# Grouping the tiled attention matmuls of a Nystromformer + multiplicative FFN kernel, with two batches' hidden values in one tile

## Chip, cores and metric

The kernel runs on one core of one Trainium2 chip. The metric is device time in microseconds (us) of one execution; several executions are compared by their median.

## What is computed

The reference is an attention in Nystrom form over 8 batches, 8 heads, 576 positions and 64 channels, followed by a feed-forward net whose third and fourth weight are applied one after the other.

```python
q_lm, k_lm = means of q, k over groups of 18 positions      # 32 landmarks
A  = softmax(q    @ k_lm.T / 8)                              # 576 x 32
Bm = softmax(q_lm @ k_lm.T / 8)                              # 32 x 32
C  = softmax(q_lm @ k.T    / 8)                              # 32 x 576
Z  = Bm.T / (norm_1(Bm) * norm_inf(Bm) + 1e-6)
for _ in range(6):
    Z = 2 * Z - Z @ Bm @ Z
x  = (A @ Z @ C @ v)            # heads side by side: 4608 x 512
out = ((x @ w1) * (x @ w2) @ w3) @ w_out
```

Inputs and output are float32.

## The kernel before

**The stages.** `fold` multiplies w3 by w_out once into `w34` (64 products of three 128x512 matmuls each, L507, with transposes of w3 in between, L494). The attention of batch 0 is woven between these products. After that a loop over the eight batches `b` does two things at once: it applies the feed-forward net to batch b, and it advances the attention of batch b+1. The attention of a batch is never multiplied out to x. Instead `attention` folds Z C v into the up weights: it leaves `g` = (Z C v) w1 and w2 per head group (L430) and `ahat`, the normalised A, and `up` multiplies g by ahat.

**The feed-forward part of batch b.** For each of eight 128-row slices j of the hidden layer there are two calls of `up`: w = 0 (4 matmuls of 128x288, L444; ScalarE copies the result to `a_sb`, L448) and w = 1 (4 more; VectorE multiplies it by a_sb into `ab`, L450). `down` then takes 128 rows of ab at a time; a chunk is two halves of four 128x512 matmuls (L464), and after the second half ScalarE writes `o_sb` (L470) and SyncE sends it out. 576 rows are four and a half chunks: an even batch does four chunks, and the odd batch after it does five, the first from 64 rows of the batch before and 64 of its own, as two column tiles of 64.

**The attention as a generator.** `attention` yields after each step, and the main loop calls `steps(at, n)` to place a step behind a piece of feed-forward work. TensorE executes in program order, so this placing is a schedule written by hand (`manual_schedule`). In this document the steps are named so:

| name | what TensorE does | lines |
|---|---|---|
| L | landmark sums from `parts` into `psL`, then `lm` (ScalarE), `qbd` (VectorE) | L201, L206, L208 |
| B | landmark scores, then bm and bt on VectorE | L217 to L230 |
| C0, C1 | scores of k against q landmarks, exp to `ect`, row sums `es` on GpSimd (`presum`) | L242, L246, L253 to L258 |
| R, A0 | first product of the iteration and A scores of heads 0 to 3 | L306, L292 |
| A1, V0 | A scores of heads 4 to 7, C v of heads 0 to 3 | L292, L323 |
| V1 | C v of heads 4 to 7 | L323 |
| I0 to I5 | the six iterations; the row sums of A (`denominators`) in I1, their reciprocals in I2 to I4, `rmix` in I5 | L387 to L397, L349, L357, L364 |
| Z, N0 | last product, `zt`, and `normalise(0)` to ahat | L407, L412, L371, L374 |
| N1, G | `normalise(1)` and the four pieces of g, one for each step | L371, L430 to L436 |

In the loop, L of the next batch stands at the end of the iteration before; B to I1 follow the eight `up(j, 0)` one each; the rest follow the halves of `down`.

**Buffers in PSUM.** `big` is a pool of three two-bank tiles, used by up, scores, iterations, normalise, g and every second down chunk. `small` and `acc` are one bank each. `bank` is acc in the main loop and small for batch 0. The sums and reciprocals of A (`psS`) lie in a big tile from I1 to I5.

**Queues.** SyncE's queue holds, in order: `turn_all(b+2)` (four DMA transposes, L106) at the start of an iteration, four pieces of v (L85), each held until ScalarE has written one element of its target (L84), and the output DMAs (L477). GpSimd does `presum`, two small products (`bmn`, `bmbd`) and then `landmarks` of batch b+2 (L183 to L192), between whose operations it issues the loads of q and k of batch b+3 (`qk_pieces`). For batch 1 v is one load (`load_v`) and for batch 2 q and k are two (`load_qk`).

Of the kernel before, what the change touches and what calls it, by code (L numbers as in the profile page):

```python
# [15 lines left out]
S = 576  # L16
# [15 lines left out]
def kernel(  # L32
# [163 lines left out]
    def attention(st, bank=None):  # L196
# [145 lines left out]
        ahat = []  # L342
        psS = None

        def denominators():
            ps = big()
# [6 lines left out]
            return ps  # L353

        def inverted(i):
            sl = slice(QS // 3 * i, QS // 3 * (i + 1))
            nc.vector.reciprocal(out=psS[:, 1, sl], in_=psS[:, 0, sl])  # L357

        def mixed():
            rr = psS[:, 1, 0:QS]  # L360
# [7 lines left out]
        def normalise(qd, rmix):  # L368
            psD = big()
            for c in range(4):  # L370
                nc.tensor.matmul(psD[:, c // 2, QS * (c % 2):QS * (c % 2) + QS],  # L371
                                 selc[:, qd, c, :], rmix[:, :], start=True, stop=True)
            a = pat.tile([128, 2, HS], FP16, name="ahat", bufs=4)
            nc.vector.tensor_tensor(out=a, in0=eat[qd].rearrange("p (c s) -> p c s", c=2),  # L374
                                    in1=psD[:, :, 0:HS], op=ALU.mult)
            ahat.append(a)


        for it in range(6):
            last = it == 5  # L380
# [24 lines left out]
        psZ = small()  # L405
        for qd in range(2):
# [11 lines left out]
        st["ahat"] = ahat  # L418


        g = st["g"] = pat.tile([128, 2, 2, DF], FP16, name="gt")
        for n in range(2):
            for w in range(2):
                psG = big()
                fs = slice(512 * n, 512 * n + 512)
                for i in range(2):
                    for h in range(4):
                        for qd in range(2):
                            rs = slice(64 * qd, 64 * qd + 64)
                            nc.tensor.matmul(psG[32 * h:32 * h + 32, qd, :], zt[rs, i, h, :],  # L430
                                             wup[rs, h, w, fs], start=(i == 0), stop=(i == 1),
                                             tile_position=(64 * qd, 32 * h))
                if w == 0:
                    nc.scalar.activation(out=g[:, :, w, fs], in_=psG, func=AXF.Copy, scale=1.0 / ZS)  # L434
                else:
                    nc.vector.tensor_scalar(out=g[:, :, w, fs], in0=psG, scalar1=1.0 / ZS,  # L436
                                            scalar2=None, op0=ALU.mult)
                yield

    def up(st, j, w):  # L440
        p = big()
        for qd in range(2):
            for c in range(2):
                nc.tensor.matmul(p[:, c, 0:HS], st["g"][:, qd, w, 128 * j:128 * j + 128],  # L444
                                 st["ahat"][qd][:, c, :], start=(qd == 0), stop=(qd == 1))
        if w == 0:
            st["a_sb"] = po.tile([128, 2, HS], FP16, name="a_sb", bufs=2)
            nc.scalar.copy(out=st["a_sb"], in_=p[:, :, 0:HS])  # L448
        else:
            nc.vector.tensor_tensor(  # L450
                out=st["ab"][:, j, :].rearrange("p (c s) -> p c s", c=2),
                in0=st["a_sb"], in1=p[:, :, 0:HS], op=ALU.mult)


    rows = out.rearrange("(b p g) f -> b g p f", b=B, g=6)

    def down(srcs, half, hold, bank):
        if half == 0:
            hold["ps"] = bank()
        pso = hold["ps"]  # L460
        for j in range(4 * half, 4 * half + 4):
            o = 0
            for _, ab, s0, sz in srcs:
                nc.tensor.matmul(pso[o:o + sz, :], ab[:, j, s0:s0 + sz], w34[:, j, :],  # L464
                                 start=(j == 0), stop=(j == 7),
                                 tile_position=(0, o))
                o += sz
        if half == 1:
            o_sb = po.tile([128, DM], FP32, name="o_sb")
            nc.scalar.activation(out=o_sb, in_=pso[:, :], func=AXF.Copy,  # L470
                                 scale=1.0 / (X64 * X64))
            o = 0
            for b, _, s0, sz in srcs:
                while sz:
                    gi, p0 = divmod(s0, NP)
                    n = min(sz, NP - p0)
                    nc.sync.dma_start(out=rows[b, 2 * (gi % 3) + gi // 3, p0:p0 + n, :],  # L477
                                      in_=o_sb[o:o + n, :])
                    o, s0, sz = o + n, s0 + n, sz - n


    def fold(pf, wof, w3f, wsp, warm_up):
# [58 lines left out]
    with tc.tile_pool(name="pf", bufs=2) as pf:  # L541
# [64 lines left out]
        turn_all(1)  # L606
        steps(fd, 6)
        at = attention(sts[0])
        for n, m in enumerate((2, 2, 2, 2, 2, 2, 2, 1, 1, 1, 1, 1, 1, 1, 2, 2, 2, 2, 2, 1)):
            steps(at)  # L610
            if n == 1:
                load_w3(7)
                load_v(sts[1], 1)
            elif n == 4:
                landmarks(sts[1], 1)
                load_qk(sts[2], 2)
                landmarks(sts[1], 0)
            steps(fd, m)
        steps(at, 30)
        steps(fd, 64)  # L620
    pab = ctx.enter_context(tc.tile_pool(name="pab", bufs=3))
    at = attention(sts[1], acc)
    steps(at)


    for b in range(B):
        st = sts[b]
        ab = st["ab"] = pab.tile([128, 8, S], FP16, name="ab")
        if b + 2 < B:
            turn_all(b + 2)  # L630
        if b % 2 == 0:
            chunks = [[(b, ab, 128 * t, 128)] for t in range(4)]
        else:
            chunks = [[(b - 1, sts[b - 1]["ab"], 512, 64), (b, ab, 0, 64)]]
            chunks += [[(b, ab, 64 + 128 * t, 128)] for t in range(4)]
# [50 lines left out]
```

## Time and profile before

| what | value |
|---|---|
| median of 8 runs | 289.14 us (287.84 to 292.28) |
| the profiled execution | 290.02 us |
| its span, first to last instruction | 288.0 us |
| TensorE busy share of the span | 95% |
| VectorE, ScalarE, GpSimd | 58%, 46%, 53% |
| batch 0's `up` begins | 73.36 us after the span's start |
| batch 7's `up` begins | 265.87 us |

The profiled execution spends 2.0 us outside its span. A row of the timeline gives start and length in us, engine, line, operation, output and inputs, shapes and count; the bracket is the idle time before it and what ended it. A matmul's length includes its way through the array, so the cost of a group is read from the start of one group to the start of the next.

### The profile page before, as it was taken

How to read it: one execution, taken by the hardware profiler on the slowest of the kernel's cores; microseconds unless marked ns; L12 is line 12 of the kernel's file. 1: busy time of each engine (PE TensorE's matmuls, PEld its weight loads, DVE VectorE, ACT ScalarE, POOL GpSimd, SP SyncE). 2: the span in 40 equal slices, each digit the busy share in tenths (PEclk: the TensorE clock that was granted, in tenths of full speed). 3: DMA queues.
4: the chain of work that ended last, by engine and by line, in shares of the span. 5: the costliest groups of instructions: out<-in, count | busy, mean ns of one | idle time of the engine just before them, and what ended most of it. 6: DMA issues, size and time to landing. Idle time of an engine off the chain costs nothing.

```text
span 288.0 us, 9554 instructions
## 1 busy us (share of the span) xinstructions
PE 274.1 (95%) x4028; PEld 151.0 (52%) x4028; DVE 167.2 (58%) x430; ACT 131.8 (46%) x231; POOL 152.3 (53%) x200
## 2 busy tenths in 40 slices
PE   7999999979999999999999999999999999999994
PEld 3455455434674476437644753475467436744641
DVE  7743242644566576647666765576576656765720
ACT  3653333222652564257426733573376246525531
POOL 1809642692299459915992898089819921400000
PEclk9999999999999999999999999999999999999998
DMA  7999999999329899998799989699997422012124
GB/s 255 293 239 269 211 236 171 211 206 179 60 84 194 159 154 165 192 180 160 173 173 194 154 203 182 134 139 229 167 165 172 132 83 76 2 36 77 36 54 128
DMA packets 61898, 45.57 MB, mean 158 GB/s; under 512 B 35488, under 2 KB 53920, under 8 KB 61856
## 3 DMA queue, kind: packets, MB, share of 16 engines
q1 hardware_dynamic: 47344, 32.12, 48.6%
q0 software_dynamic: 13792, 11.54, 28.5%
q10 hardware_dynamic: 720, 1.31, 1.2%
q8 instruction: 31, 0.51, 0.7%
q14 instruction: 11, 0.09, 0.1%
HBM read 38.80 MB, written 9.44 MB: 167 GB/s over the span
## 4 chain that ended last, share of the span: by engine, by line
PE 77%; DVE 7%; ACT 7%; POOL 4%; issue 2%; DMA 1%; ACTq 0%; DVEq 0%; POOLq 0%
PE big L444 18%; PE acc L464 13%; PE big L464 11%; PE acc L507 9%; PE big L430 6%; DVE ab L450 5%; PE big L387 4%; ACT a_sb L448 3%; PE small L323 2%; PE acc L323 2%; PE small L507 2%; PE big L371 2%; PE big L242 1%; ACT lm L206 1%; PE big L494 1%
## 5 line engine op out<-in xcount | busy, mean ns | idle before, releaser
L444 PE MATMUL big<-ahat,gt 128*128 128x288 f16 x512 | 74.0, 286 | 2.8 <-ACT a_sb L448 1.7
L450 DVE TENSOR_TENSOR ab<-a_sb,big 128x576 f16<-128x576 f16 x64 | 48.0, 751 | 16.9 <-PE big L444 8.9
L448 ACT CAST a_sb<-big 128x576 f16<-128x576 f32 x64 | 41.0, 640 | 35.9 <-PE big L444 35.1
L444 PEld LDWEIGHTS <-gt 128*128 128x128 f16 x512 | 47.1, 98 | 18.8 <-issue 3.9
L253 POOL TENSOR_TENSOR t<-ect 96x384 f32<-96x384 f32 x16 | 16.0, 997 | 65.5 <-ACT ect L246 64.8
L507 PE MATMUL acc<-wsp,w3t 128*128 128x512 f16 x168 | 41.6, 380 | 0.9 <-ACT w L510 0.7
L464 PEld LDWEIGHTS <-ab 128*128 128x128 f16 (+1 forms) x320 | 24.0, 100 | 32.3 <-issue 9.7
L464 PE MATMUL acc<-w,ab 128*128 128x512 f16 (+1 forms) x192 | 40.9, 382 | 0.0
L464 PE MATMUL big<-w,ab 128*128 128x512 f16 x128 | 32.8, 381 | 0.0
L436 DVE TENSOR_SCALAR gt<-big 128x1024 f16<-128x1024 f32 x16 | 19.6, 1225 | 20.2 <-PE big L430 20.2
L183 POOL TENSOR_TENSOR tr<-qkT 128x768 f32<-128x768 f16 x16 | 26.3, 1644 | 8.3 <-DMA qkT<-qkn 7.8
L507 PEld LDWEIGHTS <-w3t 128*128 128x128 f16 x192 | 17.7, 98 | 20.5 <-issue 3.2
L470 ACT ACTIVATE o_sb<-acc 128x512 f32<-128x512 f32 x20 | 11.9, 597 | 34.3 <-PE acc L464 34.3
L184 POOL TENSOR_TENSOR tr<-tr,qkT 128x768 f32<-128x768 f32 x16 | 26.3, 1641 | 1.3
L500 DVE SCALAR_TENSOR_TENSOR w3t<-big,w3t 128x512 f16<-128x512 f32 x16 | 11.0, 690 | 18.6 <-ACT w3t L499 18.6
L430 PE MATMUL big<-wup,zt 64*32 64x512 f16 x512 | 19.6, 381 | 1.7 <-issue 1.7
L434 ACT ACTIVATE gt<-big 128x1024 f16<-128x1024 f32 x16 | 16.4, 1024 | 7.0 <-PE big L430 7.0
L470 ACT ACTIVATE o_sb<-big 128x512 f32<-128x512 f32 x16 | 9.6, 597 | 20.8 <-PE big L464 20.8
L499 ACT ACTIVATE w3t<-big 128x512 f16<-128x512 f32 x16 | 9.5, 594 | 11.2 <-PE big L494 6.3
L246 ACT ACTIVATE ect<-big 96x768 f32<-96x768 f32 x16 | 12.9, 807 | 3.3 <-PE big L242 2.9
L190 POOL TENSOR_TENSOR o<-o,tr 128x256 f32<-128x256 f32 x16 | 12.9, 804 | 1.3
L374 DVE TENSOR_TENSOR ahat<-eat,big 128x576 f16<-128x576 f16 x16 | 12.0, 749 | 1.4 <-PE big L371 1.4
(310 smaller groups left out, 365.6 us busy)
## 6 DMA issues: line engine op xcount, KB each, us to landing
vt<-in_v_dram SPq DMA_DIRECT2D x24, 288.0 KB, 3.5
out_dram<-o_sb SPq DMA_DIRECT2D x24, 192.0 KB, 2.8
w3f<-in_moe_w_dram SPq DMA_DIRECT2D x6, 512.0 KB, 6.9
out_dram<-o_sb SPq DMA_DIRECT2D x24, 128.0 KB, 3.6
qkn<-in_k_dram POOLq DMA_DIRECT2D x10, 288.0 KB, 5.4
qkn<-in_q_dram POOLq DMA_DIRECT2D x10, 288.0 KB, 5.3
vt<-in_v_dram SPq DMA_DIRECT2D x2, 1152.0 KB, 12.2
wup<-in_moe_w_dram POOLq DMA_DIRECT2D x4, 512.0 KB, 32.4
```

Source lines behind the costliest of these rows:

```text
L183: eng.tensor_tensor(out=tr, in0=x[:, :, 0, :], in1=x[:, :, 1, :], op=ALU.add)
L184: eng.tensor_tensor(out=tr, in0=tr, in1=x[:, :, 2, :], op=ALU.add)
L253: nc.gpsimd.tensor_tensor(out=t3[0:NP], in0=e[:, :, 0:3, :], in1=e[:, :, 3:6, :], op=ALU.add)
L430: nc.tensor.matmul(psG[32 * h:32 * h + 32, qd, :], zt[rs, i, h, :], wup[rs, h, w, fs], start=(i == 0), stop=(i == 1), tile_position=(64 * ...
L434: nc.scalar.activation(out=g[:, :, w, fs], in_=psG, func=AXF.Copy, scale=1.0 / ZS)
L436: nc.vector.tensor_scalar(out=g[:, :, w, fs], in0=psG, scalar1=1.0 / ZS, scalar2=None, op0=ALU.mult)
L444: nc.tensor.matmul(p[:, c, 0:HS], st["g"][:, qd, w, 128 * j:128 * j + 128], st["ahat"][qd][:, c, :], start=(qd == 0), stop=(qd == 1))
L448: nc.scalar.copy(out=st["a_sb"], in_=p[:, :, 0:HS])
L450: nc.vector.tensor_tensor(out=st["ab"][:, j, :].rearrange("p (c s) -> p c s", c=2), in0=st["a_sb"], in1=p[:, :, 0:HS], op=ALU.mult)
L464: nc.tensor.matmul(pso[o:o + sz, :], ab[:, j, s0:s0 + sz], w34[:, j, :], start=(j == 0), stop=(j == 7), tile_position=(0, o))
L470: nc.scalar.activation(out=o_sb, in_=pso[:, :], func=AXF.Copy, scale=1.0 / (X64 * X64))
L507: nc.tensor.matmul(psW[j][:, :], turned[j, c // 4][:, a, c % 4, :], wsp[:, b, c, :], start=(c == 0 and a + b == 0), stop=(c == 7 and a == 1))
```

## The change

R, A0, A1, V0 and V1 become one step, so that all their matmuls follow each other. The four pieces of g become two steps of two. `normalise(0)` moves into I5 and `normalise(1)` behind Z. The row sums of A and their reciprocals move from a big tile into unused columns of V0's bank (`psX`, pool small) and from I1 to I0. L moves from the end of the iteration before into the first `up`. The table that places the steps in the main loop changes: five steps among the ups and I0 behind them, so the iterations I1 to I5 stand among the halves of down. `ab` becomes one tile for two batches, so that a chunk of down across the border is an ordinary chunk of 128 rows. For batch 0, R and V1 use big tiles. Batch 1's v is loaded in four gated pieces, and batch 2's q and k in four pieces between the landmark operations of batch 1.

```diff
-        psR = bank()
+        side = acc if bank is acc else (lambda: big()[:, 0, :])
+        psR = side()
...
         scores_a(0)
-        yield
         scores_a(1)
...
-        cv(0, es0, small())
+        psX = small()
+        cv(0, es0, psX)
+        cv(1, es1, side())
         yield
-        cv(1, es1, bank())
-        yield
...
-                    nc.tensor.matmul(ps[32 * c:32 * c + 32, 0, 0:QS],
+                    nc.tensor.matmul(psX[32 * c:32 * c + 32, 208:208 + QS],
...
-            if it == 1:
-                psS = denominators()
-            elif it in (2, 3, 4):
-                inverted(it - 2)
+            if it == 0:
+                denominators()
+            if it < 3:
+                inverted(it)
+            elif it == 3:
+                rmix = mixed()
             elif it == 5:
-                rmix = mixed()
+                normalise(0)
             yield
...
-        normalise(0, rmix)
+        normalise(1)
         yield
-        normalise(1, rmix)
...
                     nc.vector.tensor_scalar(out=g[:, :, w, fs], in0=psG, scalar1=1.0 / ZS,
                                             scalar2=None, op0=ALU.mult)
-                yield
+            yield
...
-            o = 0
-            for _, ab, s0, sz in srcs:
-                nc.tensor.matmul(pso[o:o + sz, :], ab[:, j, s0:s0 + sz], w34[:, j, :],
-                                 start=(j == 0), stop=(j == 7),
-                                 tile_position=(0, o))
-                o += sz
+            nc.tensor.matmul(pso[:, :], ab[:, j, t0:t0 + 128], w34[:, j, :],
+                             start=(j == 0), stop=(j == 7))
...
-        for n, m in enumerate((2, 2, 2, 2, 2, 2, 2, 1, 1, 1, 1, 1, 1, 1, 2, 2, 2, 2, 2, 1)):
+        for n, m in enumerate((2, 2, 2, 3, 3, 2, 1, 1, 1, 1, 2, 2, 3, 3)):
             steps(at)
             if n == 1:
                 load_w3(7)
-                load_v(sts[1], 1)
             elif n == 4:
-                landmarks(sts[1], 1)
-                load_qk(sts[2], 2)
-                landmarks(sts[1], 0)
+                pieces = qk_pieces(sts[2], 2)
+                landmarks(sts[1], 1, pieces=pieces)
+                landmarks(sts[1], 0, pieces=pieces)
+            if 3 < n < 8:
+                load_v_piece(sts[1], 1, n - 4, ident[0:NP, 0:1])
             steps(fd, m)
...
     at = attention(sts[1], acc)
-    steps(at)
...
-        ab = st["ab"] = pab.tile([128, 8, S], FP16, name="ab")
+        if b % 2 == 0:
+            ab = pab.tile([128, 8, 2 * S], FP16, name="ab")
+        st["ab"], st["t0"] = ab, S * (b % 2)
...
             up(st, j, 0)
-            steps(at, 1)
+            steps(at, (1, 1, 1, 0, 1, 0, 1, 0)[j])
...
+        steps(at, 1)
         nxt = attention(sts[b + 2], acc) if b + 2 < B else iter(())
...
-            down(chunks[n // 2], n % 2, hold, bank)
-            steps(at, 2 if n == 6 and nd == 8 else 1)
+            down(ab, b - b % 2, chunks[n // 2], n % 2, hold, bank)
+            steps(at)
         steps(at, 30)
-        steps(nxt)
         at = nxt
```

More of the change, by code (lines that the diff above doesn't have):

```diff
@@ L333, in cv @@
                                     scalar1=rcr[:, 0:1], scalar2=None, op0=ALU.mult)
-        cv(0, es0, small())
+        psX = small()
+        cv(0, es0, psX)
+        cv(1, es1, side())
         yield
-        cv(1, es1, bank())
-        yield
-        ahat = []
-        psS = None
         def denominators():
-            ps = big()
             for qd in range(2):
                 for c in range(4):
-                    nc.tensor.matmul(ps[32 * c:32 * c + 32, 0, 0:QS],
+                    nc.tensor.matmul(psX[32 * c:32 * c + 32, 208:208 + QS],
                                      onesq[:, qd].rearrange("p a b h -> p (a b h)"),
@@ L352, in denominators @@
                                      start=(qd == 0), stop=(qd == 1), tile_position=(0, 32 * c))
-            return ps
+        rr = psX[:, 352:352 + QS]
         def inverted(i):
             sl = slice(QS // 3 * i, QS // 3 * (i + 1))
-            nc.vector.reciprocal(out=psS[:, 1, sl], in_=psS[:, 0, sl])
+            nc.vector.reciprocal(out=rr[:, sl], in_=psX[:, 208 + sl.start:208 + sl.stop])
         def mixed():
-            rr = psS[:, 1, 0:QS]
             rhi = pat.tile([128, QS], FP16, name="rhi", bufs=1)
@@ L366, in mixed, with normalise @@
             return rmix
-        def normalise(qd, rmix):
+        ahat = st["ahat"] = []
+        def normalise(qd):
             psD = big()
@@ L414, in attention @@
                                        op0=ALU.mult, op1=ALU.subtract)
-        normalise(0, rmix)
+        normalise(1)
         yield
-        normalise(1, rmix)
-        st["ahat"] = ahat
         g = st["g"] = pat.tile([128, 2, 2, DF], FP16, name="gt")
@@ L450, in up, with down @@
             nc.vector.tensor_tensor(
-                out=st["ab"][:, j, :].rearrange("p (c s) -> p c s", c=2),
+                out=st["ab"][:, j, st["t0"]:st["t0"] + S].rearrange("p (c s) -> p c s", c=2),
                 in0=st["a_sb"], in1=p[:, :, 0:HS], op=ALU.mult)
     rows = out.rearrange("(b p g) f -> b g p f", b=B, g=6)
-    def down(srcs, half, hold, bank):
+    def down(ab, b0, t0, half, hold, bank):
         if half == 0:
@@ L472, in down @@
             o = 0
[L473 to L479, printed above, removed]
+            while o < 128:
+                gi, p0 = divmod((t0 + o) % S, NP)
+                n = min(128 - o, NP - p0)
+                nc.sync.dma_start(out=rows[b0 + (t0 + o) // S, 2 * (gi % 3) + gi // 3, p0:p0 + n, :],
+                                  in_=o_sb[o:o + n, :])
+                o += n
     def fold(pf, wof, w3f, wsp, warm_up):
@@ L620 @@
         steps(fd, 64)
-    pab = ctx.enter_context(tc.tile_pool(name="pab", bufs=3))
+    pab = ctx.enter_context(tc.tile_pool(name="pab", bufs=2))
     at = attention(sts[1], acc)
-    steps(at)
     for b in range(B):
         st = sts[b]
-        ab = st["ab"] = pab.tile([128, 8, S], FP16, name="ab")
+        if b % 2 == 0:
+            ab = pab.tile([128, 8, 2 * S], FP16, name="ab")
+        st["ab"], st["t0"] = ab, S * (b % 2)
         if b + 2 < B:
             turn_all(b + 2)
[L631 to L635, printed above, removed]
+        chunks = range(0, 512, 128) if b % 2 == 0 else range(512, 2 * S, 128)
         for j in range(8):
             up(st, j, 0)
-            steps(at, 1)
+            steps(at, (1, 1, 1, 0, 1, 0, 1, 0)[j])
             if b + 2 < B and j > 3:
```

## Prediction

> **What bounds the kernel now.** I read the page's busy shares and its chain of waits first, then the sums by stretch (one for each batch), then the timeline of TensorE in one even batch, where each start can be set against the matmuls in front of it.
>
> ```profile
> PE 274.1 (95%) x4028; PEld 151.0 (52%) x4028; DVE 167.2 (58%) x430; ACT 131.8 (46%) x231; POOL 152.3 (53%) x200
> PE 77%; DVE 7%; ACT 7%; POOL 4%; issue 2%; DMA 1%; ACTq 0%; DVEq 0%; POOLq 0%
> ```
>
> TensorE is busy 95% of the span and 77% of the chain that ends last; no other engine passes 58%. So idle TensorE is at most some 14 us, and what can be won beyond that is the price of its own groups.
>
> ```profile
> 184.30:210.98 26.68, 25.98 (x457) 14.83 (x456) 17.28 (x46) 14.03 (x26) 18.92 (x24) 1.00 0.92 169
> 210.98:239.63 28.65, 28.06 (x474) 15.44 (x472) 18.91 (x46) 13.88 (x26) 16.25 (x20) 1.00 0.62 136
> 265.87:288.00 22.13, 17.51 (x120) 9.99 (x112) 7.26 (x9) 8.27 (x14) 0.00 (x0) 0.96 0.26 71
> ```
>
> Stretch, length, busy of PE, PEld, DVE, ACT, POOL, clock, DMA. An even batch takes 26.68, an odd one 28.65; from 73.36 to 265.87 the seven batches that carry an attention take 192.51.
>
> ```profile
> 184.30 0.65 PE L444 MATMUL big<-ahat,gt 128*128 128x288 f16 x4
> 185.25 0.22 PE L217 MATMUL acc<-lm 64*32 64x32 f16 x8 [0.29 <-ACT lm L206]
> 185.40 1.15 PE L444 MATMUL big<-ahat,gt 128*128 128x288 f16 x8
> 186.39 0.69 PE L242 MATMUL big<-qbd,qkT 128*96 128x64 f16 x12
> 187.28 1.14 PE L444 MATMUL big<-ahat,gt 128*128 128x288 f16 x8 [0.20 <-ACT a_sb L448]
> ...
> 190.02 0.33 PE L306 MATMUL acc<-bt 32*32 32x32 f32 x16
> 190.28 0.32 PE L292 MATMUL big<-qkT,lm 64*32 64x288 f16 x8
> 190.53 1.16 PE L444 MATMUL big<-ahat,gt 128*128 128x288 f16 x8
> 191.61 0.32 PE L292 MATMUL big<-qkT,lm 64*32 64x288 f16 x8
> 191.86 0.88 PE L323 MATMUL small<-vt,ect 96*32 96x64 f32 x48
> 192.55 0.22 PE L328 MATMUL small<-ones,es 96*32 96x1 f32 x8
> 192.70 1.15 PE L444 MATMUL big<-ahat,gt 128*128 128x288 f16 x8
> ...
> 206.48 0.63 PE L430 MATMUL big<-wup,zt 64*32 64x512 f16 x16
> 207.04 1.04 PE L464 MATMUL big<-w,ab 128*128 128x512 f16 x4
> 208.01 1.06 PE L430 MATMUL big<-wup,zt 64*32 64x512 f16 x32
> 209.00 1.04 PE L464 MATMUL big<-w,ab 128*128 128x512 f16 x4
> ```
>
> Prices, from start to start. Eight up matmuls take 0.99 in front of L242 (185.40 to 186.39) but 1.08 in front of a tiled group (190.53 to 191.61). Four down matmuls take 0.97 in front of a tiled group (207.04 to 208.01), and in the last batch, with nothing between, eight take 1.73 (278.41 to 280.14), so 0.865 for four. Entering a tiled group thus costs about 0.10. One g group of 16 is 0.56 (206.48 to 207.04), two together 0.99 and not 1.12. R is 0.26, an A group 0.25, a C v group 0.69 + 0.15.
>
> **Waits now.** Between the ends so computed and the next starts I find four in each batch: B 0.36 (its lm), then up(1,1) 0.37 (a buffer held by a_sb), and two at I0 and I1, 195.72 to 196.21 and 197.28 to 197.78, 0.16 and 0.17 above the 0.33 that an iteration takes before a down half (199.52 to 199.85). The last two are big tiles not yet free. Sum 1.06.
>
> **The change, part by part.**
>
> R, A0, A1, V0, V1 in one step. Two of three entries go: 2 x 0.10. A1 behind A0 finds the same tiling, and the eight tiles of one group start within 0.02 of each other, so I take 0.12 (288 columns at the rate of an up matmul) for one of the two 0.25: 0.13. V1 behind V0: 0.10, an estimate of the same size as an entry. Sum 0.43 per batch.
>
> Here the Trainium skill speaks against it: "TensorEngine Tiling (Array Packing)", section Key Properties, says that a change of tiling mode, not just of tile, drains TensorE. R is 32x32, A 64x32, C v 128x32: side by side they still change mode at each border. Counting mode changes by that rule, at 0.10 each, the up part falls from eight to four, 0.40, which is the same sum by another route. But it also forbids more: the first A and the first C v must keep their full prices 0.25 and 0.84, and they do in my sum. If A1 and V1 got nothing, 0.20 would be left.
>
> G by twos. An even batch has two single groups and one pair now: 2 x (0.56 + 0.10) + 1.09 = 2.41; two pairs are 2.18, so 0.23. An odd batch has four singles, 2.64: 0.46. The skill warns at this place too: the same page, section PSUM Bottleneck, says that tiling speeds up TensorE but not the emptying of PSUM. A pair's evictions are 1.02 on ScalarE (L434) and 1.23 on VectorE (L436). By the rule alone two pairs cost 2 x 1.23 = 2.46, more than now. In the trace a down half stands between pairs, so pairs start 0.99 + 0.97 = 1.96 apart, above 1.23; I keep 2.18, and the rule is the slow rival below.
>
> ab in one tile. The two column tiles of 64 run side by side: eight of them took 0.99 (225.23 to 226.22), four whole ones 0.97. Worth 0.04 in an odd batch, 0.12 in the last, whose first chunk took 1.85 against 1.73. Sum 0.2. The output DMAs stay the same pieces.
>
> Row sums in psX, from I0. The matmuls and reciprocals (3 x 0.46) are the same; VectorE does them after the copies that the next iteration waits for, and 1.30 per step leaves it room. What changes is that no big tile is held: the two waits 0.16 and 0.17 should go.
>
> L in the first up, iterations behind the ups. I carried one even batch through by hand, with ups of 0.49, ScalarE starting an eviction 0.7 and VectorE 0.77 after an up's first matmul (188.50 after 187.77; 198.84 after 198.08), 0.65 and 0.75 for them, and a buffer free 0.05 later, using the buffers that the built program gives. From up(0,0) = 0: L 0.49, up(0,1) 0.92, up(1,0) 1.41, B 2.00, up(1,1) 2.15, up(2,0) 2.80, C0 3.29, up(2,1) 4.18, up(3,0) 4.92. VectorE sets this: qbd 1.89 to 2.57, ab(0) to 3.24, B's four small operations to 4.20, ab(1) to 4.87. Waits here: 0.16 + 0.37 + 0.25 = 0.78. Later up(5,1) waits 0.14 (exp of C1) and A1 0.11 (ab(5)). Sum 1.03, against 1.06: the old waits go and others of their size come. The merged step starts at 9.28, up(6,1) at 11.60, I0 at 13.17, the next up(0,0) at 26.02 against 26.68. In it V1 needs es of heads 4 to 7 at 11.45; GpSimd has it at 10.3.
>
> GpSimd's landmarks start at 11.3 instead of 9.0 (193.27 after 184.30), take 14.2 (193.27 to 207.45) and end at 25.5; L needs them at 26.5. Slack falls from 3.1 to 1.0 in an even batch, 2.7 in an odd one; covered, but thinly. Loads for the batch after next move with them by 2.3; their transposes have until 11.3 of the next batch.
>
> The head. Four entries fewer and two g pairs: 0.43 + 0.46, and two short waits (52.78, 56.95) of 0.3: 1.2. The four ScalarE gates (0.19 each) lie on an engine 46% busy, and run before 52.5, while SyncE's queue stands in the transposes of batch 1 until 52.51: the pieces of v go out when the one load did. Four loads of 0.70 on GpSimd in place of 0.84 + 0.78 put the landmarks of batch 1 from 66.5 to about 68; L comes after 70.
>
> ```profile
> 62.00 0.40 PE L430 MATMUL big<-wup,zt 64*32 64x512 f16 x6
> 64.10 0.61 PE L430 MATMUL big<-wup,zt 64*32 64x512 f16 x10 [1.70 <-issue]
> ```
>
> TensorE stops for 1.70 inside a group, waiting for nothing that the profile shows, while v and q, k of two batches land; the trace's DMA records have a 16 KB instruction fetch at 61.40, 1.3 long. It may go (-1.70, as in all later batches, whose loads are pieces) or stay (0; the same bytes cross the same microseconds). Neither row is nearer: half, 0.85.
>
> **Sum.** Loop 4 x 0.66 + 3 x 0.89 = 5.3; tile of two batches 0.2; head 1.2; fetch 0.85; less 0.15 per batch, 1.05, for waits that mean durations hide. 6.5. The 2.0 outside the span stay. The profiled 290.02 becomes 283.5; it lies 0.9 above the median 289.14, so on that scale 282.6.
>
> **Rivals.**
> Merged groups save only their entries (no gain in A1 and V1): 8 x 0.23 = 1.8 less, 284.4. For it: the mode rule. Against it: the g pair, 0.99.
> Slower: the seam between g and ups fills with evictions. The second pair's second group needs the buffer of the first pair's second group; by my times it is free at 25.48 and wanted at 25.46. Then lm and qbd queue behind these evictions too, where L stood ahead of them before. If VectorE's 1.23 is exposed whole in each of seven batches: +8.6, 291.2. It decides from 1.06 per batch (6.5 + 0.9, by seven). Against it: VectorE stands idle 0.8 before that eviction.
> GpSimd late: landmarks 2.5 beyond my time cost 4 x 1.5 = 6, 288.6, no change. For it: no idle time there now but the wait for ect (64.8). Against: its rows repeat within 1%.
>
> **Chances.** Forecast 0.66, rivals 0.14, 0.12, 0.08. About 0.3% (0.9 us) is what a measurement of this kernel can tell. The first two are faster; the third case is slower; the fourth lies about no change. Faster 0.82, same 0.06, slower 0.12. The range goes down to 280.0 (fetch stall gone wholly, 0.85; no hidden waits, 1.05; 0.1 less wait per batch) and up to 288.9: no gain in A1 and V1 1.8, stall stays 0.85, 0.3 more wait per batch 2.1; that is 287.4, and the rest takes in the GpSimd case.
>
> **What would show it.** Right: even batches near 26.1, odd near 27.9; V1 starting about 0.75 after V0, no single g group; I0 to up or down in 0.33 and row sums without a wait; batch 0's ups at 71 to 72. Wrong: up(3,0) later than 5.5 after up(0,0), L waiting for parts on GpSimd, the second g pair broken by a wait for VectorE, or a new idle stretch marked issue.

## The result and the profile after

The changed kernel takes 285.39 us as the median of 12 runs (283.65 to 288.05); the kernel before, in 33 runs beside it, 289.11 us (287.54 to 292.32). The ratio is 0.9878, with a 95% interval of 0.9849 to 0.9907: faster by 1.2%, or 3.7 us. The forecast was 6.5 us. The profiled execution took 284.39 us with a span of 282.6.

The page of the kernel after, its busy shares, the chain that ended last by engine, and the row of the instruction fetches (queue, packets, MB, share):

```profile
PE 270.1 (96%) x3996; PEld 152.2 (54%) x3996; DVE 165.6 (59%) x430; ACT 130.2 (46%) x235; POOL 153.3 (54%) x202
...
q8 instruction: 31, 0.51, 0.8%
...
PE 81%; DMA 7%; POOL 5%; ACT 3%; issue 2%; DVE 1%; ACTq 1%; POOLq 0%
```

TensorE is still the bound, with a larger share of the chain (81% for 77%). The shares of VectorE and ScalarE in it have shrunk from 7% each to 1% and 3%, while that of DMA has grown from 1% to 7%, in the first loads of the head. The fetch row becomes important below: 0.51 MB in 31 fetches is 16 KB for each.

The sums by stretch of the kernel after, with the columns as before (stretch, length, PE, PEld, DVE, ACT, POOL, clock, DMA, GB/s):

```profile
97.17:126.47 29.30, 27.60 (x473) 15.80 (x465) 19.09 (x46) 14.11 (x26) 19.07 (x25) 1.00 0.96 175
...
180.38:206.72 26.34, 25.73 (x457) 14.87 (x455) 16.64 (x44) 13.21 (x26) 18.89 (x24) 1.00 0.93 178
206.72:234.38 27.66, 27.41 (x472) 15.70 (x465) 19.09 (x46) 14.12 (x26) 16.29 (x20) 1.00 0.83 151
234.38:260.34 25.96, 25.71 (x457) 14.90 (x456) 16.65 (x44) 12.69 (x22) 4.78 (x8) 1.00 0.17 46
```

The even batch that took 26.68 takes 26.34, the odd one 27.66 instead of 28.65. But batches of one kind no longer agree: odd ones take 29.30, 27.77 and 27.66, even ones 25.85, 26.14, 26.34 and 25.96. In the kernel before, batches 2 and 4 agreed within 0.01, as did 3 and 5. The seven batches together take 189.03 (192.51 before).

The timeline of TensorE of the kernel after, in batch 0, an even one (start, length, line, output and inputs, shapes, count, idle time before):

```profile
71.32 0.65 PE L439 MATMUL big<-ahat,gt 128*128 128x288 f16 x4
71.81 0.59 PE L201 MATMUL small<-parts,iit 128*128 128x512 f16 x2
72.24 1.14 PE L439 MATMUL big<-ahat,gt 128*128 128x288 f16 x8
73.31 0.22 PE L217 MATMUL acc<-lm 64*32 64x32 f16 x8
73.47 1.29 PE L439 MATMUL big<-ahat,gt 128*128 128x288 f16 x8
74.59 0.69 PE L242 MATMUL big<-qbd,qkT 128*96 128x64 f16 x12
75.53 2.21 PE L439 MATMUL big<-ahat,gt 128*128 128x288 f16 x16 [0.25 <-ACT a_sb L443]
...
80.46 0.33 PE L307 MATMUL acc<-bt 32*32 32x32 f32 x16
80.71 0.56 PE L292 MATMUL big<-qkT,lm 64*32 64x288 f16 x16
81.20 0.88 PE L323 MATMUL small<-vt,ect 96*32 96x64 f32 x48
...
81.95 0.86 PE L323 MATMUL acc<-vt,ect 96*32 96x64 f32 x48
...
82.78 1.64 PE L439 MATMUL big<-ahat,gt 128*128 128x288 f16 x12
...
94.20 1.06 PE L425 MATMUL big<-wup,zt 64*32 64x512 f16 x32
95.19 1.04 PE L457 MATMUL big<-w,ab 128*128 128x512 f16 x4
96.16 1.08 PE L425 MATMUL big<-wup,zt 64*32 64x512 f16 x32
97.17 0.66 PE L439 MATMUL big<-ahat,gt 128*128 128x288 f16 x4
```

L stands in the first up (71.81), with no wait for GpSimd in front of it. R, both A groups and both C v groups follow each other in 2.32 us (80.46 to 82.78). The two pairs of g take 0.99 and 1.01 with a down half of 0.97 between, and no bracket shows a wait for VectorE there. One short wait is left in the rows shown, 0.25 for a_sb at 75.53.

The batches that came out too long show why in the same view. Batch 1's merged step, and a g group in the head:

```profile
60.09 1.04 PE L425 MATMUL big<-wup,zt 64*32 64x512 f16 x28
61.80 0.40 PE L425 MATMUL big<-wup,zt 64*32 64x512 f16 x4 [0.66 <-issue]
...
107.88 0.86 PE L323 MATMUL acc<-vt,ect 96*32 96x64 f32 x48
108.55 0.21 PE L328 MATMUL acc<-ones,es 96*32 96x1 f32 x6
110.22 0.20 PE L328 MATMUL acc<-ones,es 96*32 96x1 f32 x2 [1.46 <-issue]
```

TensorE stops inside groups of equal matmuls, four and two before their ends, and waits for nothing that the profile shows. There are four such stops in this execution: 0.61 at 52.36, 0.66 at 61.80, 1.46 at 110.22 and 0.37 at 193.97, together 3.1. The profile before had one, 1.70 at 64.10, in the head. Counted over all TensorE's records in order (matmuls, weight loads, semaphore instructions), the four stops lie whole multiples of 256 apart, to within one record: they end at records 961, 1218, 2753 and 5570, each 193 or 194 more than a multiple of 256.

### The profile page after: what moved, and what is told of

Same layout as the page of the kernel before. It is cut to its first block, busy times and chain, and to the rows that moved or that the text cites. A ratio compares the mean times of both kernels' runs of the same rounds, so it can differ in the third digit from the quotient of the medians.

```text
span 282.6 us, 9486 instructions
## 1 busy us (share of the span) xinstructions
PE 270.1 (96%) x3996; PEld 152.2 (54%) x3996; DVE 165.6 (59%) x430; ACT 130.2 (46%) x235; POOL 153.3 (54%) x202
## 4 chain that ended last, share of the span: by engine, by line
PE 81%; DMA 7%; POOL 5%; ACT 3%; issue 2%; DVE 1%; ACTq 1%; POOLq 0%
PE big L439 23%; PE acc L457 13%; PE big L457 11%; PE acc L497 8%; PE big L382 6%; PE big L425 5%; DMA qkn<-in_q_dram 4%; DMA wof<-in_moe_w_out_dram 2%; ACT a_sb L443 2%; PE small L323 2%; PE big L367 2%; PE acc L323 2%; PE big L242 2%; PE big L292 1%; PE big L484 1%
## 5 line engine op out<-in xcount | busy, mean ns | idle before, releaser
L439 PEld LDWEIGHTS <-gt 128*128 128x128 f16 x512 | 48.4, 98 | 21.4 <-issue 7.4
L497 PE MATMUL acc<-wsp,w3t 128*128 128x512 f16 x168 | 40.6, 379 | 1.1 <-ACT w L500 0.5
L457 PE MATMUL acc<-w,ab 128*128 128x512 f16 x160 | 40.3, 381 | 0.0
L457 PEld LDWEIGHTS <-ab 128*128 128x128 f16 x288 | 24.0, 98 | 29.0 <-issue 4.2
L425 PE MATMUL big<-wup,zt 64*32 64x512 f16 x512 | 17.4, 380 | 0.7 <-issue 0.7
L208 DVE TENSOR_TENSOR qbd<-lm,par 128x512 f16<-128x512 f16 x8 | 5.5, 692 | 15.2 <-ACT lm L206 15.2
```

Source lines behind the costliest of these rows:

```text
L457: nc.tensor.matmul(pso[:, :], ab[:, j, t0:t0 + 128], w34[:, j, :], start=(j == 0), stop=(j == 7))
L497: nc.tensor.matmul(psW[j][:, :], turned[j, c // 4][:, a, c % 4, :], wsp[:, b, c, :], start=(c == 0 and a + b == 0), stop=(c == 7 and a == 1))
```

## Theories

**Code blocks (my theory).** TensorE's instructions come in fetches of 16 KB, and the stops lie multiples of 256 records apart, which makes 64 bytes for each. In the trace's DMA records the fetch of a block starts about when the block before it begins, or up to some us later. Where TensorE stops, the block's first instruction executes 2.3 to 2.7 us after the fetch's start: 107.94 for the stop that ends at 110.22, 191.64 for 193.97, 61.40 in the kernel before for 64.10. The merged step has 288 instructions in some 2.2 us. A block that lies wholly inside it is used up before the next is there: begun 106.50, used up 108.7, the next one executes at 110.22. In the loop of the kernel before the two densest blocks lasted 3.6 and 3.9. A late fetch can do the same to a block that is not dense: the block in front of the stop at 64.10 lasted 11.2, but the next one's fetch began 8.5 after it. What held that fetch back is not shown.

The Trainium skill, "Runtime: NRT & Kernel Launch", section Instruction fetch mechanics, describes the same blocks: refills of 16 KiB, the next page fetched while the current one executes. It calls the cost of a boundary "mostly hidden". The trace agrees with the size and the order; the last words hold only where a block lasts longer than its successor's way.

**Rivals.** The stops come from the DMA transposes of `turn_all`, which hold up all other queues; or the loss lies in the new schedule, as waits that the records name badly; or the gain itself is smaller, because one part of the change brought nothing.

## The experiments

Each ran on one chip beside the kernel before (289.01 for e1, e2, e3 and e8; 289.00 for e4 to e7; 290.03 for f1 to f4). "Loop" is the seven batches 0 to 6; for it one profiled execution was read.

| run | median us | ratio (95%) | batch 0 begins | loop |
|---|---|---|---|---|
| before | 289.11 | 1 | 73.36 | 192.51 |
| after | 285.39 | 0.9878 (0.9849 to 0.9907) | 71.32 | 189.03 |
| e8, after again | 285.76 | 0.9872 (0.9819 to 0.9926) | 70.85 | 192.00 |
| f3, before again | 289.89 | 1.0000 (0.9970 to 1.0030) | 73.94 | 192.50 |
| e2, after without transfers | 282.56 | 0.9765 (0.9720 to 0.9811) | 73.15 | 187.35 |
| e3, before without transfers | 290.03 | 1.0027 (0.9994 to 1.0061) | 72.25 | 192.50 |
| e1, after shifted by half a block | 292.56 | 1.0051 (1.0021 to 1.0081) | 77.56 | 190.32 |
| e7, V1 apart | 286.73 | 0.9910 (0.9879 to 0.9941) | 74.57 | 190.31 |
| f1, after without transposes | 284.52 | 0.9807 (0.9762 to 0.9851) | 70.76 | 189.07 |
| e4, before with G by twos | 289.59 | 0.9977 (0.9948 to 1.0005) | 71.59 | 190.60 |
| e5, before with A merged | 289.10 | 1.0008 (0.9979 to 1.0037) | 71.88 | 192.32 |
| e6, after with whole loads in the head | 286.46 | 0.9882 (0.9837 to 0.9928) | 69.97 | 189.68 |
| f2, after with the sums in a big tile | 286.78 | 0.9865 (0.9807 to 0.9923) | 74.03 | 190.74 |
| f4, after with the sums of es whole | 285.37 | 0.9860 (0.9810 to 0.9910) | 70.56 | 189.98 |

### Both kernels without the transfers of the loop (e2, e3)

In both kernels nothing is loaded or transposed in the loop, and the four ScalarE gates of v fall away; each batch takes the transposed q, k and the v of batch 0 or 1 again. The output is still written.

```diff
-            turn_all(b + 2)
+            sts[b + 2]["qkT"], sts[b + 2]["vt"] = st["qkT"], st["vt"]
...
-            pieces = qk_pieces(...)
+            pieces = iter(())
```

> The changed kernel without the loads of q, k and v and the transposes in the main loop: batches 2 to 7 use the transposed q, k and the v of batches 0 and 1 again, and the four gates of v are left out too. Landmarks, scores and all arithmetic are still done. Theory (code blocks come late because of the loop's transfers): no stop marked issue in the main loop, even in the batches whose blocks lie in the merged step; the seven batches take 187.0 to 187.6 instead of 189.0, and the runs scatter less than the 4.4 us of the changed kernel. Rival (late blocks have nothing to do with the transfers): the stops of 1.46 and 0.37 stay.

> The kernel before with the same transfers left out (batches 2 to 7 use the transposed q, k and the v of batches 0 and 1 again). It has no stop marked issue in the loop, so the theory of code blocks expects the seven batches at 192 to 192.5 as before, and the difference between this and the changed kernel without transfers near 5.0 in the loop: the gain of the schedule alone, of which 1.8 was lost again in the profiled execution. Rival (the gain is smaller for another reason): the difference is the same 3.5 as with transfers.

Batches 2 and 3 of the quiet changed kernel, sums by stretch (batches 4 and 5 have the same lengths):

```profile
127.31:153.27 25.96, 25.72 (x458) 14.90 (x456) 16.65 (x44) 12.70 (x22) 16.25 (x20) 1.00 0.17 46
153.27:180.93 27.66, 27.41 (x473) 15.70 (x466) 19.09 (x46) 13.58 (x22) 16.25 (x20) 1.00 0.18 48
```

With a DMA share of 0.17 the batches agree again, at 25.96 and 27.66. One stop is left in the loop, in batch 1 at 111.06, of 0.46. The loop of the kernel before is the same with transfers and without (192.50), and so, within the interval, is its whole time. The changed kernel gains 2.8 us by medians (285.39 to 282.56). So the transfers, with their gates, cost the new order of instructions about 3 us and cost the old one nothing that can be told. Without them the change is worth 7.5 (290.03 to 282.56); that this is more than the forecast 6.5 is within the intervals.

The last batch of the loop of the kernel after is a control in the same execution, since nothing is loaded in it any more:

```profile
243.62 0.33 PE L307 MATMUL acc<-bt 32*32 32x32 f32 x16
...
245.13 0.86 PE L323 MATMUL acc<-vt,ect 96*32 96x64 f32 x48
245.81 0.22 PE L328 MATMUL acc<-ones,es 96*32 96x1 f32 x8
245.96 0.30 PE L439 MATMUL big<-ahat,gt 128*128 128x288 f16 x1
```

The same step runs through in 2.34. The block inside it executes from 243.17 to 245.60, as dense as the one of batch 1, but the fetch of the next started at 242.78, 2.82 before it was needed, and TensorE did not stop.

### The same kernel, its blocks cut elsewhere (e1)

64 small matmuls, 128 instructions with their weight loads, are added behind the warm-up; everything after them moves half a block.

```diff
         warm_up(7)
+        for _ in range(64):
+            nc.tensor.matmul(psw[0:32, 0, 0:32], warm[0:32, 0:32], warm[0:32, 0:32],
+                             start=True, stop=True)
```

> The changed kernel with 64 tiny 32x32 matmuls added behind the first warm-up, which put 128 more instructions (a weight load and a matmul each) in front of TensorE's whole stream and do nothing else. Theory (code blocks): TensorE's instructions arrive in blocks of 256; the changed kernel's stops marked issue all stand at an index of 193 modulo 256, and a block that lies wholly in the merged step (288 instructions in 2.2 us) is used up before the next has come. Then the stops stay at the same index modulo 256 but move to other places: batches 0, 2, 3 and 5 have a block in the merged step now, in place of 1 and 4, and lose some 0.5 to 1.6 us each; the seven batches with an attention, 189.0 us in the changed kernel, take 190 to 192, and the whole 1 to 3 us more, part of it the tiny matmuls themselves at the start. Rival (the stops belong to that place in the program, or to chance): batch 1 keeps its stop of 1.46 us, and the loop keeps 189.0 within 0.5.

The timeline of e1, a stop in the head and one in batch 3, and the row of the granted clock in 40 slices:

```profile
47.49 0.81 PE L497 MATMUL acc<-wsp,w3t 128*128 128x512 f16 x3
52.39 1.01 PE L497 MATMUL acc<-wsp,w3t 128*128 128x512 f16 x2 [4.09 <-issue]
...
171.41 0.24 PE L343 MATMUL small<-eat,onesq 128*32 128x144 f16 x3
172.72 0.28 PE L343 MATMUL small<-eat,onesq 128*32 128x144 f16 x5 [1.06 <-issue]
...
PEclk9999999599999999999999999999999999999999
```

The stops moved: batches 1 and 4 ran nearly undisturbed (27.80 and 25.96), and stops of 0.69, 1.06 and 1.39 stand at 91.11, 172.72 and 225.81, again at places with the same remainder by 256, to within one record. So the stops go with the place in the code, not with the particular matmul that stands there. Batch 2, where one was expected too, had none (25.96): a block of 2.7 lies in its merged step, but the next fetch started 0.1 before it.

The size I had wrong. One stop in the head, right behind batch 0's merged step while the loads of the head run, kept TensorE idle for 4.1, and the granted clock was 0.50 from 50.28 to 57.11. Set against the same instructions of the kernel after, the 6.2 by which batch 0 begins later are 1.6 for the added matmuls, 4.1 for the stop and 2.3 for the slow clock behind it, less 1.8 for the two stops of the kernel after that this head does not have.

### V1 in a step of its own (e7)

```diff
         cv(0, es0, psX)
+        yield
         cv(1, es1, side())
```

The tables of steps take one more in the head and among the ups.

> The changed kernel with C v of heads 4 to 7 taken out of the merged step and put behind the eighth up (w = 0), so that no block of 256 instructions lies wholly in tiled matmuls. By the prediction's prices this costs 0.10 for the entry and 0.10 for V1 in each of eight batches, 1.6. Theory (code blocks): it takes away the stops of 1.46 and 0.37 in batches 1 and 4, so that the sum is about even: the loop 189.0 to 188.6, and no stop marked issue in it; the scatter of the runs is smaller. Rival (the stops don't hang on the merged step): the stops stay and the loop is 1.4 longer.

The loop was 0.29 longer per unstopped batch (26.14 and 27.95 for 25.85 and 27.66), and the stops did not go: 0.36 at 113.84 and 1.03 at 197.97, with two in the head (1.05 and 1.76). Two rows of its timeline:

```profile
196.28 0.66 PE L440 MATMUL big<-ahat,gt 128*128 128x288 f16 x4
197.97 0.40 PE L383 MATMUL big<-sz__3479,tz__3480 32*32 32x96 f32 x16 [1.03 <-DVE ab L446]
```

The bracket names a wait for ab. But the place has the remainder of a block's first instruction, and the same I0 begins with `[0.37 <-issue]` in the kernel after. A releaser is inferred. The ab operation ends at 197.81, 0.16 before; in e8, where this I0 carries the same bracket, at 196.04, 0.31 before it starts. So it was probably only the last semaphore that the instruction had. Parting one group is not enough: the blocks in front of the two stops lasted 3.4 and 3.7 without them, and the fetches behind them began 0.8 (and took 1.6 instead of about 1) and 2.2 late.

### Without the transposes alone (f1)

Only the transposes of later batches are left out (q and k of batches 0 and 1 are used again); the loads stay.

```diff
-            turn_all(b + 2)
+            sts[b + 2]["qkT"] = st["qkT"]
```

> The changed kernel without the DMA transposes of the main loop alone: the loads of q, k and v stay, batches 2 to 7 use the transposed q and k of batches 0 and 1 again. Theory (the transposes are what a code block waits behind): no stop at index 193 modulo 256 in batches 1 to 5, the seven batches at 187.3 to 187.8 as without any transfer. Rival (any transfer delays a block): stops of 0.4 us and more stay in batches 1 to 5 and the loop stays above 188.5.

```profile
108.00 0.21 PE L328 MATMUL acc<-ones,es 96*32 96x1 f32 x6
109.47 0.20 PE L328 MATMUL acc<-ones,es 96*32 96x1 f32 x2 [1.27 <-issue]
```

The stop of batch 1 stayed (1.27 for 1.46), another of 0.71 came at 193.46, and the loop took 189.07. The rival falls: the stops do not need the transposes. In the DMA records a fetch started behind the beginning of the block before it by 1.82 on average in batches 0 to 5 of the kernel after, by 1.58 here and by 0.90 without any loads (e2). Single fetches are 3.3 to 3.5 late even in e2, so the loads are not all that delays them; the rest stays open.

### Both kernels once more (e8, f3)

> The changed kernel once more, for a second profiled execution. Theory (code blocks): the stops stand at the same indices modulo 256 (193), but their lengths differ, since they depend on how long the block waits behind other transfers: batches 1 and 4 between 0 and 2 us each, the head between 0 and 3 in sum, and the times of the runs differ by about as much. Rival (another cause of the scatter): the stops are the same lengths within 0.2 us and the two profiled executions differ elsewhere.

> The kernel before once more, for a second profiled execution: theory (code blocks) expects its stops in the head only, 0.5 to 2 us in sum at index 193 modulo 256, none above 0.3 in the main loop, the seven batches at 192.5. Rival (the stops hit it as often as the changed kernel): stops in the loop too.

The kernel before repeats its loop to 0.01 (192.50) and has its long stop at the same matmul of the head (1.43 at 64.68), with a short one of 0.47 at 53.80. The kernel after stops at the same places with other lengths: 1.72 at 110.02 (1.46 before), a new one of 0.27 at 142.99, and 1.27 at I0 of batch 4 where there was 0.37; its loop is 3.0 longer. In the head it has 0.43 and 0.39 for 0.61 and 0.66. One row of its timeline and one of its sums by stretch:

```profile
110.02 0.22 PE L328 MATMUL acc<-ones,es 96*32 96x1 f32 x2 [1.72 <-issue]
```

```profile
110.00:125.00 15.00, 14.98 (x202) 6.71 (x209) 8.91 (x24) 3.81 (x7) 12.18 (x15) 0.89 0.93 180
```

In the 15 us behind that stop the granted clock was 0.89, where the first execution had 1.00: it was 0.50 for 3.41 us (109.86 to 113.27) and 1.00 before and after. Batch 1 took 30.96 instead of 29.30. So a stop can cost more than its own length, and one execution is a single draw of it. The medians hold such draws: of the 12 executions of the kernel after, eight have a mean granted clock of 0.996 to 1.000 and a median of 284.8, four have 0.991 to 0.994 and 287.2; 3.41 us at half clock take 0.006 off the mean.

### G by twos alone (e4), on the kernel before

```diff
                                             scalar2=None, op0=ALU.mult)
-                yield
+            yield
...
-            steps(at, 2 if n == 6 and nd == 8 else 1)
+            steps(at)
```

> The kernel before with g by twos alone (two steps of two pieces, behind two halves of down; nothing else moved). By the prediction's prices 0.23 less in an even batch, 0.46 in an odd one, 0.46 in the head: 2.8 in all, 288.9 to about 286.3. The rival that evictions of g fill the seam expects no gain or a wait for VectorE in front of the second pair.

```profile
203.58 1.06 PE L430 MATMUL big<-wup,zt 64*32 64x512 f16 x32
204.57 1.04 PE L464 MATMUL big<-w,ab 128*128 128x512 f16 x4
205.53 1.08 PE L430 MATMUL big<-wup,zt 64*32 64x512 f16 x32
206.54 1.04 PE L464 MATMUL big<-w,ab 128*128 128x512 f16 x4
```

A pair takes 0.99 and 1.01, without a wait for the evictions. An even batch became 0.23 shorter (26.68 to 26.45), an odd one 0.34 (28.65 to 28.31). The loop gained 1.9. By medians the kernel is not faster (289.59): its profiled execution, 285.74, is the fastest of 22. The clock tells a part: the mean granted clock of that execution was 0.998, and that of 17 of the other 21 only 0.991 to 0.994, where 33 of 35 of the kernel before beside them had 0.996 or more. The five executions of e4 with 0.996 or more have a median of 287.6. Why the clock fell in most of its executions stays open, since none of those was profiled.

### A and C v merged alone (e5), on the kernel before

```diff
         scores_a(0)
-        yield
         scores_a(1)
...
         cv(0, es0, small())
-        yield
-        cv(1, es1, bank())
+        cv(1, es1, side())
         yield
```

> The kernel before with R, A and both C v groups in one step alone (behind the fifth up; the row sums stay in a big tile, L stays where it was, g stays single). By the prediction's prices 0.43 less per batch, 3.4 in all. Code blocks: the merged step is 288 instructions in 2.2 us here too, so some batches should show a stop marked issue at an index of 193 modulo 256, together 1 to 3 us, and the gain in the median should be only 1 to 2.5. The rival that merged groups save only their entries expects 0.2 per batch, and A1 and V1 starting 0.25 and 0.84 after A0 and V0.

```profile
187.00 2.26 PE L443 MATMUL big<-ahat,gt 128*128 128x288 f16 x16
189.19 0.33 PE L307 MATMUL acc<-bt 32*32 32x32 f32 x16
```

An unstopped batch gained only 0.1 (26.60 and 28.56). The groups are cheaper, but the ups, which now follow each other with nothing between, take 2.19 for 16 (the 0.99 for eight of the prediction gives 1.98). The rest is about 0.09 for the entry to R and a wait of 0.14 in the middle, which ends at 188.12, just behind ScalarE's exp of C1 (to 188.07), the eviction of a big tile. So an entry saved can be lost again where the work that came between gave an eviction its time. Batch 4 stopped as the theory of code blocks has it, on the kernel before too once its code was packed:

```profile
193.40 0.90 PE L443 MATMUL big<-ahat,gt 128*128 128x288 f16 x6 [0.49 <-issue]
```

### The loads of the head (e6), the row sums (f2) and the sums of es (f4), on the kernel after

e6 loads v of batch 1 and q, k of batch 2 whole, as before; f2 puts the row sums of A and their reciprocals back into a big tile; f4 does the four column sums of es of a group (L328) as one untiled matmul behind both C v groups.

```diff
+                load_v(sts[1], 1)
...
-                pieces = qk_pieces(sts[2], 2)
-                landmarks(sts[1], 1, pieces=pieces)
+                landmarks(sts[1], 1)
+                load_qk(sts[2], 2)
```

```diff
+        psS = big()
...
-                    nc.tensor.matmul(psX[32 * c:32 * c + 32, 208:208 + QS],
+                    nc.tensor.matmul(psS[32 * c:32 * c + 32, 0, 0:QS],
```

```diff
-            for h in range(4):
-                nc.tensor.matmul(psV[32 * h:32 * h + 32, 64:65], es[0:NP, h, :], ones[0:NP, :],
-                                 start=True, stop=True, tile_position=(0, 32 * h))
...
+            nc.tensor.matmul(psV[:, 64:65], es[0:NP].rearrange("p h m -> p (h m)"), ones[0:NP, :],
+                             start=True, stop=True)
```

> The changed kernel with batch 1's v in one load and batch 2's q and k in two, as before. The prediction took half of the head's stop of 1.70 as won by the pieces. Theory now: the head's stops hang on blocks that come late behind transfers of the same bytes, so pieces change little: the same within 0.5. Rival (the pieces matter): one stop near 62 of 1.7 us or more, and 1 to 1.5 us slower.

> The changed kernel with the row sums of A and their reciprocals in a big tile again, from I0 to I3, in place of free columns of V0's bank. By the prediction's reading of the two waits at I0 and I1 (0.16 and 0.17) a held big tile costs 0.3 or more per batch: even batches 26.1 to 26.4 in place of 25.85 to 25.96, 2 to 3.5 in all. Rival (the iterations now stand behind the ups, where two big tiles are enough): no difference above 0.1 per batch.

> The changed kernel with the row sums of C (four 32-column float32 matmuls for each group) as one 128-column matmul for each group, both behind the merged step's C v: 24 instructions fewer per batch, and the merged step 264 in place of 288. Prices: 0.05 to 0.15 less per batch without stops, 0.4 to 1.2 in all; the stops stay (a block of 256 still fits into the step), at other batches since the blocks move. The theory of code blocks expects anything from 2 us less to 1 us more, with the stops' sum explaining it; the loop without stops 186.3 to 187.0.

e6: batch 0 begins at 69.97, no later than with the pieces, and this head has no stop at all. The pieces brought nothing that shows in the head. The median (286.46) lies within its interval of the kernel after.

f2: undisturbed batches take 25.85 and 27.66, exactly as with psX. The row sums hold a big tile, and nobody waits for it once the iterations stand behind the ups. Its stops (1.55 at 113.28, 0.73 at 197.57, 0.44 at 250.10) make most of the rest of its 190.74. Batch 0 begins late (74.03) behind a stop of 1.60 at 54.35 and a granted clock of 0.50 from 54.62 to 58.03.

f4: 12 matmuls fewer in each attention, 264 instructions in the merged step. Its profiled execution has one stop, 0.59 at 111.46. But the untiled pair costs more than the sixteen small ones did:

```profile
163.32 0.38 PE L329 MATMUL small<-ones,es 96*128 96x1 f32 x2
163.56 0.36 PE L329 MATMUL acc<-ones,es 96*128 96x1 f32 x2
163.78 1.63 PE L443 MATMUL big<-ahat,gt 128*128 128x288 f16 x12
```

It takes 0.46, and an undisturbed batch became 0.35 longer. Fewer stops and longer batches seem to cancel: 285.37 by the median, which the kernel after has as well. None of the versions that compute the reference beats the changed kernel by more than the intervals.

## Why the prediction was right, and where its sum was off

The direction was right and the time lay in the range; of the 6.5 us, 3.7 came. The parts:

| step of the prediction | forecast | measured |
|---|---|---|
| loop and tile of two batches, schedule alone | -5.5 | -5.8 (192.50 to 25.85 + 3 x 25.96 + 3 x 27.66 = 186.7) |
| head without stops | -1.2 | -1.8 (batch 0's start less the stops: 71.7 and 72.0 before and f3, 70.0 in after, e8 and e6) |
| stop in the head | -0.85 | about -0.3, not shown: 1.7, 1.9 and 0.6 with the head before (before, f3, e3); 1.3, 0.8, 2.4 and 0 with the head after (after, e8, e2, f1) |
| waits that mean durations hide | +1.05 | +2.3, +5.3, +3.0 in the loop (after 189.03, e8 192.00, e6 with the same loop 189.68, less 186.7) |

With the mean of the last row, 3.5, the measured parts add up to about -4.4; the medians say -3.7.

**The schedule.** Replayed by hand, an even batch was to take 26.02 and takes 25.85 to 25.96; an odd one 27.75 or so, and takes 27.66. Batch 0's ups were to begin at 71 to 72 and begin at 71.32. The single parts were less exact; that their errors cancelled was luck. G by twos was right in an even batch (0.23) and too large in an odd one (0.46 forecast, 0.34 in e4). A1 behind A0 was to cost 0.12: in the head it did (both A groups 0.37, from 43.40 to 43.77), in the loop they take 0.49, as two single ones had; why the two places differ stays open. V1 behind V0 saves 0.1, as it was given (0.75 for V0 and 0.83 for V1, where two single ones took 2 x 0.84). Merging saved little by itself (0.1 in e5), and psX nothing (f2), so by subtraction most of what remains belongs to L in the first up and the iterations behind the ups, which were not run alone. The tile of two batches brought nothing in the last batch (22.24 for 22.13).

**The term that was mis-sized** is "0.15 per batch, 1.05, for waits that mean durations hide". I had the row of the cause on the table, the 1.70 marked issue with a fetch of 16 KB beside it, and asked only whether that stop would go. I did not ask what makes a stop: that a block of code is used up sooner than the next arrives. Packing 288 instructions into 2.2 us while loads run makes such a block wherever a whole one falls into the merged step; in this kernel that is in batch 1 (and in batch 6, without loads). Batch 4 stopped too, behind a block that lies only partly in it, since the fetch began 1.5 late. The allowance would have had to be some 3.5, of which a half-clock stretch like that of e8 is a part. The profile gave what was needed: the count of instructions in the step, its time, and 2.7 from the fetch at 61.40 to the start at 64.10.

**The two executions flatter the change.** 290.02 to 284.39 is 5.6, since the first was 0.9 above its median and the second 1.0 below. In e8 and f3 it is 3.5.

**The rivals.** No wait for VectorE at the second g pair; GpSimd's landmarks are in time (L at 71.81 has no bracket, nor has any L of the loop). "Merged groups save only their entries" was half true: for A1 in the loop, without showing in the whole. What the prediction listed last as a sign of being wrong, "a new idle stretch marked issue", is what came.

## What to carry to other kernels

Before packing many small matmuls into one stretch, count the instructions (a weight load counts) and compare: 256 of them must last longer than a fetch takes to arrive, here 2.3 to 2.9 us from its start (3.0 and 3.8 at two of the stops), plus what it starts late. An "issue" bracket inside a group of equal matmuls, with stops multiples of 256 records apart, points to that stop, and it moves if the code before it changes its length, so a kernel can become faster or slower by an edit far from the stop. Judge such a change by several executions, and measure once without the transfers to see what the schedule alone is worth.

## What the runs showed of the hardware

- TensorE's stops for code: 0.3 to 1.7 us in the loop, 4.1 in the head of e1, always at the same remainder by 256 records, to within one. The fetch starts about when the block before begins, later by 0.9 on average without the loads of the loop and 1.8 with them (batches 0 to 5 of e2 and of the kernel after).
- The clock behind a stop: in three profiled executions the granted clock fell to 0.50 within a stop or just behind it, 1.6 to 2.0 us after its beginning: for 6.83 us with the stop of 4.1 (e1), for 3.41 with 1.72 (e8) and with 1.60 (f2). Behind stops of 1.46 (the kernel after), 1.70 (the kernel before) and 1.76 (e7) it stayed at 1.00. The Trainium skill, "TensorE: Matmul & The Clock Gate", Part 1, lets the clock fall after an idle window of about 3.4 us. The stretches at half clock are one and two such lengths, but the falls came sooner, and no run here shows what made them.
- Two tiled groups of the same kind side by side: two g groups take 0.99 (0.56 one alone), two C v groups 1.58 (0.84 one alone), two A groups in the loop 0.49 (0.25 one alone), that is, no less.
